# Moving the first loads of W_v to a second DMA queue, in a kernel for linear attention and a gated feed-forward layer

## The chip, the cores and the metric

The kernel runs on one core of a Trainium2 chip. A core has a matrix engine (TensorE, PE in the profile), a vector engine (VectorE, DVE), an engine for activation functions (ScalarE, ACT), a general one (GpSimd, POOL), and SyncE (SP), which here only issues DMA transfers. Each engine takes its instructions in order and they wait for each other through semaphores. SyncE and ScalarE each have a queue of DMA transfers; the transfers run on 16 DMA engines. The metric is the device time of one execution, in microseconds (us); smaller is better.

## The reference

One transformer layer on a sequence of 2048 rows of 640 numbers, in bf16: a layer norm, linear attention with 32 heads of 20 channels, a second layer norm and a gated feed-forward layer of width 1536.

```python
qkv = layernorm(x) @ wqkv                      # 640 x 1920, split into q, k, v
pq = einsum("bhsd,hdf->bhsf", q, w_phi)        # 20 x 20 for each head; the same for k
phi_q = concat(softmax(pq), softmax(-pq))      # 40 features for each head; the same for k
kv = einsum("bhsf,bhsd->bhfd", phi_k, v)
num = einsum("bhqf,bhfd->bhqd", phi_q, kv)
den = einsum("bhqf,bhf->bhq", phi_q, phi_k.sum over s) + 1e-6
h = x + (num / den) @ wo
out = h + (gelu(layernorm(h) @ w_gate) * (layernorm(h) @ w_up)) @ w_down
```

## The kernel before

The 2048 rows are 16 tiles of 128 rows; four tiles share one buffer `x_sb[b]`. A weight with 640 rows lies in SBUF as five chunks of 128 rows, so that W_v, the last third of `wqkv`, is `Wv[:, 0:5, :]`, each chunk 128 x 640 (160 KB, as is a tile of x).

The work comes in three stages: k and v of all tiles with the sums over the sequence (`kv_tile`), q and the attention's output, and the feed-forward layer. W_k and W_q are not used as they are: they are loaded transposed (`load_T`, `WkT`) and multiplied on TensorE with a block-diagonal matrix `BD` made from `w_phi` (`fold`), so that one product with the normalised x gives the features before the softmax. `BD` is made by one VectorE instruction (`bd`, L433) from `wphi` and a mask.

The order of the instructions on TensorE and SyncE is the order of the program text, and under a manual schedule around the whole kernel that of the other engines too. A DMA transfer signals one of eight semaphores, taken in turn by the order of the text; a transfer whose semaphore was used by an earlier one waits, on the issuing engine, until that one has landed.

The change is in the start. The first loads are at L189 to L198, then five transposing loads of W_k follow (L203). ScalarE issues one of them, `wphi`, and then loads its table of functions. TensorE meanwhile runs matmuls on constants (`warm`, L228). What follows is this:

- Tiles 0 and 1 are centred but not scaled (`xc`), transposed on TensorE (`tr_c`, into `LN1T`, copied by ScalarE at L165) and their scale, the reciprocal deviation, is applied later, when ScalarE moves v out of PSUM (`v_ev`, L316). The statistics of tile 0 are VectorE's (`ln_0`), those of tile 1 ScalarE's (`st_act`, L407 and L409).
- VectorE then takes the statistics of tile 2 (`ln_st(2)`), `BD`, the normalised tile 2 (`ln_ap(2)`, L156), the statistics of tile 3 with the copy of tile 2's transposes in between (`ln_st(3, between=...)`), and tile 3 after that.
- TensorE runs v of tiles 0 and 1 in parts (`v_part(t, chunks)`, L312, two matmuls of 320 columns for each chunk of W_v), with the transposes of tile 2 among them (`ln_tp(2, True)`, L164), then v of tile 2, the transposes of tile 3, and the five folds of W_k (L248), with v of tile 3 and parts of k in between.

The lines of the start that are concerned:

```python
439: st_act(1, 0)
440: xc = [ln_0(0)]
441: xc.append(xc_a(1))
442: tr_c(0)
443: tr_c(1)
444: ln_st(2, act=False, log=True)
445: bd(0, NC)
446: st_act(1, 1)
447: warm(*[P] * 4)
```

Of the kernel before, what the change touches and what calls it, by code (L numbers as in the profile page):

```python
# [17 lines left out]
def kernel(  # L18
# [12 lines left out]
    nc = tc.nc  # L31
    P = 128
    S = 2048
    D = 640
# [5 lines left out]
    NC = D // P  # L40
# [34 lines left out]
    w_v = A_wqkv.rearrange("(c p) n -> p c n", p=P)  # L75
    phi_v = A_w_phi.rearrange("h d f -> (h d) f")
# [9 lines left out]
    wphi = const.tile([P, NC, Dh], BF16, name="wphi")  # L86
# [24 lines left out]
    def gtile(name):  # L111
        return psG.tile([P, 2, 512], F32, name=name, tag="G")
# [63 lines left out]
    Wv = p1.tile([P, NC, D], BF16, name="Wv")  # L176
# [11 lines left out]
    nc.gpsimd.memset(eps, EPS)  # L188
    nc.sync.dma_start(x_sb[0][:, 0:1, :], x_v[:, 0:1, :])  # L189
    nc.sync.dma_start(x_sb[0][:, 1:2, :], x_v[:, 1:2, :])  # L190
    nc.scalar.dma_start(wphi, phi_v.rearrange("(c p) f -> p c f", p=P))
    nc.scalar.add_instruction(mybir.InstLoadActFuncSet(name=nc.get_next_instruction_name(), act_func_set_id=6))
    nc.sync.dma_start(x_sb[0][:, 2:3, :], x_v[:, 2:3, :])  # L193
    nc.sync.dma_start(Wv[:, 0:2, :], w_v[:, 0:2, 2 * D:3 * D])
    nc.sync.dma_start(Wv[:, 2:4, :], w_v[:, 2:4, 2 * D:3 * D])
    nc.sync.dma_start(x_sb[0][:, 3:4, :], x_v[:, 3:4, :])
    nc.sync.dma_start(Wv[:, 4:5, :], w_v[:, 4:5, 2 * D:3 * D])
    nc.sync.dma_start(x_sb[1][:, 0:2, :], x_v[:, 4:6, :])  # L198

    def load_T(WT, i, *ds):  # L200
# [25 lines left out]
    def warm(*cols):  # L226
        for n in cols:
            nc.tensor.matmul(wu[:, 0, 0:n], lhsT=ones[:, 0:P], rhs=ones[:, 0:n], start=True, stop=True)  # L228
# [46 lines left out]
    def ln_st(*tiles, act=True, between=None, log=False):  # L275
        for t, v in zip(tiles, ln_stats(p1, [x_sb[t // 4][:, t % 4, :] for t in tiles], "1", act, between, log)):
            lnp[t] = v

    def ln_ap(t, on_act=False, on_pe=False):
        ln = (ln_act if on_act else ln_dve)(p1, "1", *lnp[t])  # L280
        if on_pe:
            lnp[t] = ln
        else:
            transpose_to(LN1T[t // 4][:, :, t % 4 * P:(t % 4 + 1) * P], ln, False)

    def ln_tp(t, on_dve=False):
        transpose_to(LN1T[t // 4][:, :, t % 4 * P:(t % 4 + 1) * P], lnp[t], True, on_dve)

    def lnT(t, c):
        b, tl = divmod(t, 4)  # L290
        return LN1T[b][:, c, tl * P:(tl + 1) * P]
# [14 lines left out]
    def v_part(t, *cs):  # L306

        if 0 in cs:
            pv[t] = gtile("pv")
        for c in cs:  # L310
            for u in range(2):
                nc.tensor.matmul(pv[t][:, u, 0:HD], lhsT=lnT(t, c), rhs=Wv[:, c, u * HD:(u + 1) * HD],  # L312
                                 start=(c == 0), stop=(c == NC - 1))

    def v_ev(t):
        nc.scalar.activation(vS[t % NV][:, :, 1:VC].rearrange("p (u h) f -> p u h f", u=2),  # L316
                             pv[t][:, :, 0:HD].rearrange("p u (h f) -> p u h f", f=Dh), ACTF.Copy,
                             scale=lnp[t][2] if t in CT else 1.0)
# [126 lines left out]
    bd(0, NC)  # L445
    st_act(1, 1)
    warm(*[P] * 4)
    v_part(0, 0, 1)
    v_part(1, 0, 1)
    ln_ap(2, on_pe=True)  # L450
    v_part(0, 2, 3)
    root = []
    ln_st(3, act=False, between=lambda: ln_tp(2, True), log=root)
    v_part(0, 4)
    v_ev(0)
    v_part(1, 2, 3)
    root[0]()
    v_part(1, 4)
    v_ev(1)
    v_part(2, *range(NC))  # L460
    d = ident.rearrange("p (r j) -> p r j", r=4)
# [476 lines left out]
```

## Time and profile before

| | us |
|---|---|
| median of 3 runs | 272.64 |
| lowest and highest | 271.77, 272.8 |
| the profiled execution | 272.35 |
| its span, first to last instruction | 270.6 |
| TensorE busy in it | 266.1 |

The costliest group of matmuls is that of the feed-forward layer (L768, 600 matmuls). The start, with which this document deals, is the first 17 us of the span; the granted clock of TensorE is 1.00 of full speed in all the stretches shown. Times in the profile count from the start of the span. A line of the timeline has the start, the length, the engine, the line of the program, the operation, what it writes and reads, and in brackets the idle time of its engine before it with what ended it. "SPq" and "ACTq" are the issues of transfers by SyncE and ScalarE; PEld is the loading of weights into TensorE.

### The profile page before, as it was taken

To read this page: it belongs to the slowest core of one execution; us is meant where nothing else is said; L and a number is where in the kernel's file an instruction comes from. 1 tells how busy PE (TensorE), PEld (TensorE's weight loads), DVE (VectorE), ACT (ScalarE), POOL (GpSimd) and SP (SyncE) were. 2 spreads that over 40 slices of the span, in tenths; PEclk is the share of its full clock that TensorE was granted. 3 is DMA by queue.
4 is the path that set the end of the run, shared out by engine and by line. 5 is a ranking of instruction groups with operands and counts; after the bars stand their busy time and mean duration, and the time that the engine had idled before them with its cause. 6 is when DMAs were issued, how large, how long until landed. Compare 5 with 4: busy or idle time off the path is not lost.

```text
span 270.6 us, 7029 instructions
## 1 busy us (share of the span) xinstructions
PE 266.1 (98%) x2857; PEld 172.0 (64%) x2857; DVE 173.9 (64%) x347; ACT 138.6 (51%) x249; POOL 101.2 (37%) x238
## 2 busy tenths in 40 slices
PE   8999999999999999999999999999999999999995
PEld 6777777765455887788755455775555476444574
DVE  5789999996877767876566783568673332333322
ACT  5779997877789675245541356421544300322100
POOL 5448898887002335376211564014661100000000
DMA  6987489213864442432301222203222101000011
GB/s 187 206 199 169 81 210 96 46 37 85 326 201 112 157 101 55 68 78 50 51 27 51 48 50 48 50 3 75 76 46 51 24 24 51 24 0 0 4 48 48
DMA packets 45264, 22.10 MB, mean 82 GB/s; under 512 B 37808, under 2 KB 43184, under 8 KB 45232
## 3 DMA queue, kind: packets, MB, share of 16 engines
q1 hardware_dynamic: 44576, 21.64, 33.5%
q8 instruction: 22, 0.36, 0.6%
q10 hardware_dynamic: 656, 0.03, 0.2%
q14 instruction: 10, 0.08, 0.1%
HBM read 10.18 MB, written 2.62 MB: 47 GB/s over the span
## 4 chain that ended last, share of the span: by engine, by line
PE 96%; DMA 2%; SPq 0%; DVE 0%; issue 0%
PE gu L768 39%; PE pd L790 19%; PE pq L396 8%; PE pk L296 8%; PE po L708 8%; PE pv L296 7%; DMA Wv<-in_A_wqkv_dram 2%; PE kvp L374 2%; PE pv L312 2%; PE ab L619 1%; PE wa L248 1%; PE ab L586 1%; PE tp L164 0%; SPq L193 0%; SPq L190 0%; SPq L189 0%
## 5 line engine op out<-in xcount | busy, mean ns | idle before, releaser
L771 ACT ACTIVATE g<-gu 128x512 bf16<-128x512 f32 (+1 forms) x60 | 30.4, 510 | 74.0 <-PE gu L768 73.2
L774 DVE TENSOR_TENSOR GT<-gu,g 128x512 bf16<-128x512 f32 (+1 forms) x60 | 34.3, 579 | 46.8 <-PE gu L768 38.6
L768 PE MATMUL gu<-LN2T,Wg 128*128 128x512 bf16 (+1 forms) x300 | 61.8, 337 | 0.0
L768 PE MATMUL gu<-LN2T,Wu 128*128 128x512 bf16 (+1 forms) x300 | 61.8, 336 | 0.0
L790 PE MATMUL pd<-Wd,GT 128*128 128x320 bf16 (+4 forms) x396 | 53.9, 295 | 0.0
L790 PEld LDWEIGHTS <-GT 128*128 128x128 bf16 x396 | 37.6, 98 | 14.5 <-DVE GT L774 0.2
L768 PEld LDWEIGHTS <-Wu 128*128 128x128 bf16 x300 | 29.4, 98 | 22.6
L768 PEld LDWEIGHTS <-Wg 128*128 128x128 bf16 x300 | 29.1, 98 | 21.2
L296 PEld LDWEIGHTS <-LN1T 128*128 128x128 bf16 x290 | 28.0, 98 | 10.4
L355 POOL TENSOR_TENSOR E<-E,rs 128x640 bf16<-128x640 bf16 x25 | 31.7, 1295 | 4.4 <-DVE rs L351 2.8
L792 DVE TENSOR_TENSOR y<-pd,x_sb 128x320 bf16<-128x320 f32 (+4 forms) x33 | 15.8, 480 | 24.1 <-PE pd L790 24.1
L708 PE MATMUL po<-Wo,oT 128*128 128x320 bf16 x160 | 24.5, 299 | 0.0
L296 PE MATMUL pk<-Wk,LN1T 128*128 128x320 bf16 x160 | 24.4, 299 | 0.0
L396 PE MATMUL pq<-LN1T,Wq 128*128 128x512 bf16 x100 | 22.9, 379 | 0.0
L347 DVE TENSOR_REDUCE sk<-E 128x64 f32<-128x1280 bf16 x16 | 22.9, 1430 | 0.0
L401 ACT ACTIVATE Eq<-pq 128x1024 bf16<-128x1024 f32 (+1 forms) x26 | 19.9, 831 | 2.8 <-PE pq L396 2.7
L340 ACT ACTIVATE E<-pk 128x640 bf16<-128x640 f32 x28 | 19.1, 769 | 3.0 <-PE pk L296 3.0
L708 PEld LDWEIGHTS <-oT 128*128 128x128 bf16 x160 | 15.6, 98 | 7.3 <-ACT oT L165 0.2
L296 PE MATMUL pv<-Wv,LN1T 128*128 128x320 bf16 x130 | 19.8, 299 | 0.0
L151 ACT ACTIVATE ln<-x_sb,v,rstd 128x640 bf16<-128x640 bf16 x14 | 12.9, 920 | 13.0 <-POOL v L747 12.9
L396 PEld LDWEIGHTS <-Wq 128*128 128x128 bf16 x100 | 9.4, 98 | 10.3
L683 DVE TENSOR_TENSOR tt<-AB,w 128x1280 bf16<-128x1280 f32 x10 | 15.1, 1505 | 0.4 <-POOL w L676 0.3
(120 smaller groups left out, 291.4 us busy)
## 6 DMA issues: line engine op xcount, KB each, us to landing
out_dram<-y SPq DMA_DIRECT2D x15, 160.0 KB, 1.8
x_sb<-in_A_x_dram SPq DMA_DIRECT2D x6, 320.0 KB, 3.3
Wd<-in_B_w_down_dram SPq DMA_DIRECT2D x1, 1440.0 KB, 6.8
Wg<-in_B_w_gate_dram SPq DMA_DIRECT2D x1, 1152.0 KB, 7.3
Wu<-in_B_w_up_dram SPq DMA_DIRECT2D x1, 1152.0 KB, 5.6
Wo<-in_A_wo_dram SPq DMA_DIRECT2D x1, 800.0 KB, 5.0
Wg<-in_B_w_gate_dram SPq DMA_DIRECT2D x1, 768.0 KB
Wu<-in_B_w_up_dram SPq DMA_DIRECT2D x1, 768.0 KB, 9.1
```

Source lines behind the costliest of these rows:

```text
L296: nc.tensor.matmul(ps[:, u, 0:HD], lhsT=lnT(t, c), rhs=W[:, c, u * HD:(u + 1) * HD], start=(c == 0), stop=(c == NC - 1))
L340: nc.scalar.activation(Ek[t][:, s, :].rearrange("p (u f) -> p u f", u=2), pk[:, :, 0:HD], ACTF.Exp, scale=((lnp[t][2], nrstd[t]) if t in C ...
L347: nc.vector.reduce_sum(sk, Ek[t].rearrange("p s (h f) -> p (s h) f", f=Dh), axis=AX.X)
L355: eng.tensor_tensor(e, e, rs[:, s * H:(s + 1) * H, None].to_broadcast([P, H, Dh]), ALU.mult)
L396: nc.tensor.matmul(pqs[j][:, i, :], lhsT=Wq2[:, kc, c * P:(c + 1) * P], rhs=LN1T[b][:, kc, :], start=(kc == 0), stop=(kc == NC - 1))
L401: nc.scalar.activation(Eq[j][:, :, s, :], pqs[j][:, 0:len(QG[j])], ACTF.Exp, scale=(1.0, -1.0)[s])
L708: nc.tensor.matmul(pos[u], lhsT=st[t][:, c, :], rhs=Wo[:, c, u * HD:(u + 1) * HD], start=(c == 0), stop=(c == NC - 1))
L768: nc.tensor.matmul(gu[i][:, 0:n], lhsT=W[:, c, f * P:(f + 1) * P], rhs=LN2T[b][:, c, a0:a1], start=(c == 0), stop=(c == NC - 1))
L771: nc.scalar.activation(g[:, 0:n], gu[0][:, 0:n], ACTF.Gelu_apprx_tanh)
L774: nc.vector.tensor_tensor(st[b, "g", f][:, a0:a1], gu[1][:, 0:n], g[:, 0:n], ALU.mult)
L790: nc.tensor.matmul(pd[:, 0:f1 - f0], lhsT=st[b, "g", f][:, tl * P:(tl + 1) * P], rhs=Wd[:, f, f0:f1], start=(f == 0), stop=(f == NF - 1), ...
L792: nc.vector.tensor_tensor(y[:, f0:f1], pd[:, 0:f1 - f0], x_sb[b][:, tl, f0:f1], ALU.add)
```

## The change

Two things change. ScalarE issues the first four chunks of W_v, in two transfers, instead of `wphi`; SyncE issues x tiles 0, 1 and 2, the last chunk of W_v, `wphi`, tile 3 and the rows of tiles 4 and 5. And TensorE takes all five chunks of v of tile 0 ahead of v of tile 1, with tile 0's `v_ev` right after it. The number of instructions and of bytes is the same; SyncE issues one transfer fewer, ScalarE one more.

```diff
     nc.sync.dma_start(x_sb[0][:, 0:1, :], x_v[:, 0:1, :])
     nc.sync.dma_start(x_sb[0][:, 1:2, :], x_v[:, 1:2, :])
-    nc.scalar.dma_start(wphi, phi_v.rearrange("(c p) f -> p c f", p=P))
+    nc.scalar.dma_start(Wv[:, 0:2, :], w_v[:, 0:2, 2 * D:3 * D])
+    nc.scalar.dma_start(Wv[:, 2:4, :], w_v[:, 2:4, 2 * D:3 * D])
     nc.scalar.add_instruction(mybir.InstLoadActFuncSet(name=nc.get_next_instruction_name(), act_func_set_id=6))
     nc.sync.dma_start(x_sb[0][:, 2:3, :], x_v[:, 2:3, :])
-    nc.sync.dma_start(Wv[:, 0:2, :], w_v[:, 0:2, 2 * D:3 * D])
-    nc.sync.dma_start(Wv[:, 2:4, :], w_v[:, 2:4, 2 * D:3 * D])
+    nc.sync.dma_start(Wv[:, 4:5, :], w_v[:, 4:5, 2 * D:3 * D])
+    nc.sync.dma_start(wphi, phi_v.rearrange("(c p) f -> p c f", p=P))
     nc.sync.dma_start(x_sb[0][:, 3:4, :], x_v[:, 3:4, :])
-    nc.sync.dma_start(Wv[:, 4:5, :], w_v[:, 4:5, 2 * D:3 * D])
     nc.sync.dma_start(x_sb[1][:, 0:2, :], x_v[:, 4:6, :])
```

```diff
     warm(*[P] * 4)
-    v_part(0, 0, 1)
+    v_part(0, *range(NC))
+    v_ev(0)
     v_part(1, 0, 1)
     ln_ap(2, on_pe=True)
-    v_part(0, 2, 3)
     root = []
     ln_st(3, act=False, between=lambda: ln_tp(2, True), log=root)
-    v_part(0, 4)
-    v_ev(0)
-    v_part(1, 2, 3)
+    v_part(1, 2, 3, 4)
     root[0]()
-    v_part(1, 4)
     v_ev(1)
     v_part(2, *range(NC))
```

## The prediction

> **What bounds the kernel now.** I read the page first (busy time, chain that ended last), then TensorE's waits, the chain in order of time, and the timeline of the first 17 us.
>
> ```profile
> span 270.6 us, 7029 instructions
> PE 266.1 (98%) x2857; PEld 172.0 (64%) x2857; DVE 173.9 (64%) x347; ACT 138.6 (51%) x249; POOL 101.2 (37%) x238
> ```
>
> ```profile
> PE pv L312 <- DMA Wv<-in_A_wqkv_dram: 0.9, 1, 0.9
> PE wu L228 <- PEq L922: 0.8, 1, 0.8
> ```
>
> TensorE is busy for 98% of the span and waits twice: 0.8 us for the program to begin and 0.9 us for the first chunks of W_v. The second wait is all that an earlier W_v can remove. The chain in order of time (start, length, what) shows the place, and that TensorE sets the end from there on:
>
> ```profile
> 2.18 5.18 DMA Wv<-in_A_wqkv_dram
> 7.36 0.04 issue
> 7.41 1.79 PE pv L312 x12
> 9.20 0.28 PE tp L164 x5
> 9.47 2.44 PE pv L312 x18
> 11.92 0.28 PE tp L164 x5
> 12.20 0.98 PE wa L248 x18
> ```
>
> So the first chunks, issued fourth on SyncE at 2.18, landed at 7.36. From 7.41 every piece begins where the last ended; whatever is late to one of these pieces by less than TensorE moves up costs nothing, and what is later eats the gain.
>
> **What stands before the v matmuls.** The timeline (start, length, engine, line; in brackets the idle time before) of x tiles 0 and 1:
>
> ```profile
> 1.28 1.28 ACT L192 ACT_TABLE_LOAD   x1 [1.28 <-PEq L922]
> 3.27 0.89 DVE L121 BATCH_NORM_STATS2 statsc<-x_sb 128x6 f32<-128x320 bf16 x2 [0.64 <-DMA x_sb<-in_A_x_dram]
> 4.01 0.74 ACT L407 ACTIVATE sqa<-x_sb 128x640 bf16<-128x640 bf16 x1 [1.44 <-DMA x_sb<-in_A_x_dram]
> 4.87 0.39 DVE L424 TENSOR_SCALAR xc<-x_sb,va 128x640 bf16<-128x640 bf16 x1
> 5.63 1.29 ACT L165 COPY LN1T<-tp 128x640 bf16<-128x640 bf16 x2 [0.37 <-PE tp L164]
> 5.92 0.63 PE L228 MATMUL wu<-const-bfloat16-1.0 128*128 128x128 bf16 x4
> ```
>
> Tile 1 landed at 4.01. ScalarE's statistic of tile 1 stands in its queue ahead of tile 0's copy, and TensorE transposes both tiles and runs four warm-up matmuls, until 6.55 (5.92 + 0.63), before the first v matmul. So v starts no sooner than 2.54 us after tile 1 lands, and no sooner than W_v.
>
> **The change, part by part.**
>
> *ScalarE's queue.* One issue more there (some 0.48 us, as on SyncE) moves the table load from 1.28 to about 1.76, ending at 3.04; ScalarE's next work began at 4.01. Hidden; without that 0.97 us of cover it would cost its 0.48.
>
> *The start of v.* 320 KB of W_v now travel beside x tiles 0 and 1, and w_phi no longer does. The rates of the transfers (last two columns: busy DMA engines as a share, GB/s), and w_phi's queue in the first 4 us:
>
> ```profile
> 1.75:2.50 0.75, 0.75 (x10) 0.75 (x9) 0.45 (x6) 0.75 (x1) 0.61 (x5) 1.00 0.73 176
> 2.50:3.50 1.00, 1.00 (x12) 1.00 (x11) 0.32 (x2) 0.07 (x1) 0.80 (x6) 1.00 1.13 268
> 3.50:5.00 1.50, 1.45 (x15) 1.19 (x13) 1.38 (x5) 0.99 (x3) 0.63 (x13) 1.00 0.79 195
> 5.00:7.50 2.50, 1.65 (x15) 1.48 (x15) 2.15 (x6) 2.07 (x7) 0.52 (x2) 1.00 1.00 336
> ```
>
> ```profile
> q10 hardware_dynamic: 656, 0.03, 11.2%
> ```
>
> W_v's 327,680 bytes at 336 GB/s are 0.98 us; w_phi's 656 small packets are 11.2% of 4 us, 0.45 us. Tile 1 therefore lands between 0.45 earlier (W_v fills only gaps; the share of 0.73 to 0.79 shows that there are some) and 0.98 later (no gap is filled, no credit). I take 0.98 - 0.45 = 0.53 later, since both transfers have the same size and start together: 4.54, and v at 4.54 + 2.54 = 7.08, 0.33 us sooner than 7.41. The bounds are 6.1 (in truth 6.55, as tile 0 has its own chain) and 7.53. All the later W_v chunks are wanted 0.5 and 1.1 us after that, and stand ahead of w_phi, whose landing is treated next.
>
> The Trainium skill (DMA: Bandwidth & Descriptors, "Issuing engines are not separate DMA queues") speaks against the change: transfers from different engines run on the same 16 DMA engines and interleave, so that issuing from two saves only the issue time. Taken at its strictest it gives the upper bound for tile 1, v at 7.53, and nothing gained at this place. No row of before can show it, as only w_phi came from ScalarE.
>
> *w_phi.* BD needs it, and BD stands in VectorE's queue ahead of the normalised tile 2, the statistics of tile 3 and all that follows:
>
> ```profile
> 6.62 0.94 DVE L433 TENSOR_TENSOR BD<-wphi,hmask 128x800 bf16<-128x800 bf16 x1
> 7.48 0.44 DVE L156 TENSOR_SCALAR ln<-x_sb,mv,rstd 128x640 bf16<-128x640 bf16 x1
> 8.61 0.49 DVE L121 BATCH_NORM_STATS2 stats<-x_sb 128x6 f32<-128x320 bf16 x1 [0.68 <-DMA x_sb<-in_A_x_dram]
> 9.51 0.49 DVE L165 COPY LN1T<-tp 128x640 bf16<-128x640 bf16 x1 [0.41 <-PE tp L164]
> 9.92 0.48 DVE L121 BATCH_NORM_STATS2 stats<-x_sb 128x6 f32<-128x320 bf16 x1
> 10.44 0.21 DVE L125 BATCH_NORM_AGGREGATE mv<-stats 128x2 f32<-128x12 f32 x1
> 11.25 0.45 DVE L156 TENSOR_SCALAR ln<-x_sb,mv,rstd 128x640 bf16<-128x640 bf16 x1 [0.24 <-ACT rstd L132]
> 11.76 0.45 PE L164 MATMUL tp<-ident,ln 128*128 128x128 bf16 x5
> 12.26 0.48 DVE L165 COPY LN1T<-tp 128x640 bf16<-128x640 bf16 x1
> ```
>
> ```profile
> wphi<-in_A_w_phi_dram ACTq DMA_DIRECT2D x1, 25.0 KB, 2.8
> ```
>
> Before, w_phi landed 2.8 after its issue at 0.79, by 3.6, three microseconds early. Now it is fifth on SyncE, behind x tiles 0 to 2 and the last chunk, while ScalarE's queue carries four more: 1280 KB are ahead of it or beside it, exactly what stood up to x tile 3 before (three tiles, four chunks, a tile), which landed at 8.61. With the same use of the DMA engines w_phi lands at 8.61: the upper bound. For the lower bound I stream from 2.5 at 336 GB/s, after 132 KB (0.75 us at 176): 1.34 MB are through at 6.1, and with the 0.8 that tile 1 needed (its and tile 0's 328 KB were through by about 3.2 at the rates above, against 4.01) 6.9. I take the middle, 7.75.
>
> From w_phi's landing W to tile 3's transposes, by differences of starts above: BD 0.86, tile 2's ln 0.44 and 0.05 to its transposes, 0.50 to its copy (11.76 to 12.26), 0.41 to the second statistic, 0.52 to the aggregate, 0.81 to tile 3's ln, 0.51 to its transposes: W + 4.10. For 7.75 that is 11.85. TensorE would be there at 7.08 + (11.76 - 7.41) = 11.43. So it waits 0.42, and the 0.33 won is more than returned: it stands 0.09 later than before. W = 7.66 is break-even.
>
> *SyncE's queue.* In the built program the DMAs share eight semaphores in turn, so the ninth transfer, x rows 4 and 5 (L198 in both), waits until the first on its semaphore has landed. Before, that was w_phi (3.6, and SyncE came to it at 4.15: no stall). Now it is W_v's first pair, and the five W_k transposes stand behind it:
>
> ```profile
> 4.15 0.43 SPq L198 DMA_DIRECT2D x_sb<-in_A_x_dram  x1
> 4.63 7.69 SPq L203 DMA_TRANSPOSE WkT<-in_A_wqkv_dram  x5
> 15.65 0.43 PEld L248 LDWEIGHTS <-WkT 128*128 128x128 bf16 x6
> ```
>
> ```profile
> 11.04 1.28 SPq L203 DMA_TRANSPOSE WkT<-in_A_wqkv_dram  x1
> ```
>
> ```profile
> WkT<-in_A_wqkv_dram SPq DMA_TRANSPOSE x1, 4.5
> ```
>
> ```profile
> L203 SPq DMA_TRANSPOSE WkT<-in_A_wqkv_dram x5: 1266/1276/1891, 4.6 to 11.0; - x5
> ```
>
> The last transpose, issued at 11.04, lands 4.5 later at 15.54, and its weights are loaded at 15.65: 0.11 us of slack. One issue fewer would bring SyncE to L198 at 3.67. If W_v's pair lands at 4.99 (4.01 + 0.98, the bytes of both tiles and of the pair; bounds: 4.01, as fast as two tiles alone, and 0.79 + 5.18 = 5.97, its present time from issue), L198 is 0.84 later than at 4.15. Of the 7.69 us for five transposes, 5 x 1.28 + 4 x 0.05 = 6.6 are needed; 1.1 are in longer issues, which I read as full rings that a later start relieves. So the last transpose shifts by -0.26 to +0.84; I take the middle, +0.3: 15.84, and 0.19 us of TensorE's time.
>
> *Sum.* The stalls follow each other on one engine, so the last one decides: of -0.33 at the start of v, +0.09 at tile 3 and +0.19 at the last fold, +0.19 is left. The profiled execution took 272.35 (1.75 outside the span): 272.54. It lies 0.29 below the median of 272.64; I say 272.6.
>
> The order of v itself (tile 0 whole, then tile 1) costs nothing: the same 20 matmuls, and 14 rather than 12 of them ahead of tile 2's transposes, which favours a late tile 2 by 0.27 us (2 x 0.136, from 18 in 2.44); this is in the W chain.
>
> **Rivals.**
> 1. *The gain is kept.* x and W_v fill each other's gaps, w_phi lands by 7.0, the last transpose lands 0.26 sooner or more: v at 7.0 to 6.55, and 0.37 (0.11 of slack and 0.26) to 0.86 off: 271.5 to 272.0, say 271.75. For it: shares of 0.73 and 0.79 while nothing else held the engines. Against it: the skill's rule, and that three gates must open together. Chance 0.2.
> 2. *w_phi is late* (other side): at 8.61 tile 3's transposes come at 12.71, 0.95 late: 273.3. It decides from 7.66 on. Against it: two queues may use the engines better. Chance 0.2.
> 3. *SyncE stalls behind W_v's pair* (other side): at 5.97 and no relief, the transposes shift by 1.82, the last fold waits 1.71: 274.05. It decides from 4.26 on without relief, 5.4 with it. Against it: the pair is alone in its queue. Chance 0.2.
>
> **How the numbers follow.** The forecast has 0.4, and a range of its own of 272.2 to 273.0 (the ends of the shift at the last fold). The range of 271.6 to 274.1 takes in most of rival 1, rival 2, and half of rival 3. Half a per cent, about what a measurement of this kernel can tell from no change, is 1.36 us. Faster by that (under 271.28) is out of reach of 0.86 us off 272.35 but for scatter: 0.04. Slower by it (over 274.0) needs rival 3 at its upper end, or rivals 2 and 3 together: 0.18. The rest, 0.78, is within.
>
> **What would show it.** TensorE's wait for W_v of 0.9 gone or under 0.3; L407's wait for x longer than 1.44 and its start near 4.5; BD starting at 7.75 with a wait for w_phi; TensorE waiting some 0.4 us at tile 2's or 3's transposes; SyncE idle ahead of L198 till about 5; the last fold late. If BD starts by 7.0 and the fold's weights are there, I am wrong towards rival 1; if tile 1 lands past 5, the start of v itself is a loss.

## The result, and the profile after

The changed kernel is slower. Over all runs of this measurement, 6 of each:

| | before | changed |
|---|---|---|
| median, us | 271.84 | 274.05 |
| lowest and highest | 271.57, 272.8 | 273.62, 275.62 |
| span of the profiled execution | 270.6 | 273.9 |

The ratio is 1.0095, with a 95% interval of 1.0072 to 1.0118: 2.2 us by the medians. The six runs fall into two groups: four of 273.6 to 274.1 and two of 275.5 and 275.6. The profiled one is of the second group (275.62), so it shows one thing that most runs do not have.

TensorE's waits in the profile of the changed kernel (who waited for whom, us in total, times, longest):

```profile
PE pd L787 <- DVE GT L771: 1.3, 1, 1.3
PE wu L228 <- PEq L919: 0.8, 1, 0.8
PE tp L164 <- DVE xc L272: 0.7, 1, 0.7
PE tp L164 <- DVE xc L424: 0.2, 1, 0.2
```

The wait for W_v is gone. Two small waits ahead of the transposes of tiles 0 and 1 have come, and a wait of 1.3 us at a place that no line of the diff touches: the first matmul of the down projection (`pd`), some 100 us later. It waits for `GT`, which VectorE makes from the gate and up products `gu`. The same place in the kernel before, then in the changed kernel:

```profile
103.69 2.62 PE L790 MATMUL pd<-Wd,GT 128*128 128x326 bf16 x18
```

```profile
106.92 2.62 PE L787 MATMUL pd<-Wd,GT 128*128 128x326 bf16 x18 [1.33 <-DVE GT L771]
```

Here is TensorE's timeline of the start:

```profile
5.49 0.72 PE L164 MATMUL tp<-ident,xc 128*128 128x128 bf16 x5 [0.67 <-DVE xc L272]
6.41 0.71 PE L164 MATMUL tp<-ident,xc 128*128 128x128 bf16 x5 [0.20 <-DVE xc L424]
6.92 0.63 PE L228 MATMUL wu<-const-bfloat16-1.0 128*128 128x128 bf16 x4
7.34 3.46 PE L312 MATMUL pv<-Wv,LN1T 128*128 128x320 bf16 x14
10.64 0.44 PE L164 MATMUL tp<-ident,ln 128*128 128x128 bf16 x5
10.92 2.34 PE L312 MATMUL pv<-Wv,LN1T 128*128 128x320 bf16 x16
13.36 0.45 PE L164 MATMUL tp<-ident,ln 128*128 128x128 bf16 x5
```

v starts at 7.34, where it started before (7.41). But its first 14 matmuls take 3.46 us, against 2.34 for the 16 that follow, and tile 3's transposes come at 13.36, not 11.76: 1.60 late. The durations of one v matmul, as least, median and most ns, say why (the kernel before first):

```profile
L312 PE MATMUL pv<-Wv,LN1T x30: 296/299/299, 7.4 to 11.6; 128*128 128x320 bf16 x30
```

```profile
L312 PE MATMUL pv<-Wv,LN1T x30: 299/299/474, 7.3 to 13.0; 128*128 128x320 bf16 x30
```

474 ns where the others take 299: in this run TensorE was still at its slow rate, as in the warm-up (matmuls of 128 columns take 311 ns there, and also in the transposes and the four warm-up matmuls right ahead of v; at the full rate they take about 220). The granted clock in the profile stands at 1.00 all the same.

What is behind the waits for xc is the loads. The timeline of the changed kernel (SPq and ACTq are issues):

```profile
0.79 0.46 ACTq L191 DMA_DIRECT2D Wv<-in_A_wqkv_dram  x1
1.28 0.49 ACTq L192 DMA_DIRECT2D Wv<-in_A_wqkv_dram  x1
3.88 0.89 DVE L121 BATCH_NORM_STATS2 statsc<-x_sb 128x6 f32<-128x320 bf16 x2 [1.25 <-DMA x_sb<-in_A_x_dram]
4.69 0.33 SPq L198 DMA_DIRECT2D x_sb<-in_A_x_dram  x1
5.10 0.74 ACT L407 ACTIVATE sqa<-x_sb 128x640 bf16<-128x640 bf16 x1 [2.02 <-DMA x_sb<-in_A_x_dram]
7.45 0.94 DVE L433 TENSOR_TENSOR BD<-wphi,hmask 128x800 bf16<-128x800 bf16 x1
```

Tile 0 lands 0.6 later than before (3.88 against 3.27) and tile 1 1.1 later (5.10 against 4.01). SyncE is held at L198 until W_v's first pair has landed, at 4.69. BD runs at 7.45 without a wait for w_phi.

### The profile page after: what moved, and what is told of

Read it like the earlier page. It is cut to its first block, busy times and chain, and to the rows that moved or that the text cites. A ratio compares the mean times of both kernels' runs of the same rounds, so it can differ in the third digit from the quotient of the medians.

```text
span 273.9 us, 7029 instructions
## 1 busy us (share of the span) xinstructions
PE 267.9 (98%) x2857; PEld 172.5 (63%) x2857; DVE 174.1 (64%) x347; ACT 138.8 (51%) x249; POOL 101.4 (37%) x238
## 4 chain that ended last, share of the span: by engine, by line
PE 95%; DVE 2%; DMA 1%; issue 1%; ACT 0%; SPq 0%
PE gu L765 37%; PE pd L787 19%; PE pq L396 8%; PE pk L296 8%; PE po L705 8%; PE pv L296 6%; PE kvp L374 2%; DMA x_sb<-in_A_x_dram 1%; PE ab L616 1%; PE pv L312 1%; PE wa L248 1%; PE ab L583 1%; PE tp L164 1%; DVE tt L680 1%; DVE GT L771 0%
## 5 line engine op out<-in xcount | busy, mean ns | idle before, releaser
L296 PEld LDWEIGHTS <-LN1T 128*128 128x128 bf16 x290 | 28.0, 98 | 10.4
L340 ACT ACTIVATE E<-pk 128x640 bf16<-128x640 f32 x28 | 18.5, 729 | 3.2 <-PE pk L296 3.2
```

Source lines behind the costliest of these rows:

```text
L296: nc.tensor.matmul(ps[:, u, 0:HD], lhsT=lnT(t, c), rhs=W[:, c, u * HD:(u + 1) * HD], start=(c == 0), stop=(c == NC - 1))
L340: nc.scalar.activation(Ek[t][:, s, :].rearrange("p (u f) -> p u f", u=2), pk[:, :, 0:HD], ACTF.Exp, scale=((lnp[t][2], nrstd[t]) if t in C ...
```

## The experiments

Each ran beside the kernel before on the same chip. "High" counts the runs more than 1.2 us above the lowest run of the same kernel; the kernel before has 7 such runs of 89 itself. The ratio is not that of the two medians, so the two can differ by some 0.1 to 0.2%.

| run | median, us | before beside it | ratio, 95% interval | high |
|---|---|---|---|---|
| changed kernel | 274.05 | 271.84 | 1.0095 (1.0072 to 1.0118) | 2 of 6 |
| e1, last chunk after tile 2 | 272.22 | 271.66 | 1.0038 (1.0022 to 1.0054) | 4 of 12 |
| e2, loads only | 272.17 | 271.66 | 1.0019 (1.0007 to 1.0032) | 1 of 11 |
| e3, order only | 274.19 | 271.66 | 1.0092 (1.0079 to 1.0105) | 0 of 4 |
| e4, longer warm-up | 273.75 | 271.66 | 1.0076 (1.0063 to 1.0089) | 0 of 5 |
| g1, changed, other PSUM tile | 272.33 | 271.54 | 1.0024 (0.9998 to 1.005) | 2 of 11 |
| g2, before, other PSUM tile | 273.1 | 271.54 | 1.0049 (1.0031 to 1.0068) | 0 of 11 |
| g3, x split over queues | 271.83 | 271.54 | 1.0007 (0.9988 to 1.0026) | 0 of 11 |
| g4, changed, both mended | 272.32 | 271.54 | 1.0023 (1.0004 to 1.0041) | 0 of 11 |
| h1, table before W_v | 272.85 | 271.94 | 1.0035 (1.0014 to 1.0057) | 6 of 12 |
| h2, W_v after the table | 272.58 | 271.88 | 1.0029 (1.0016 to 1.0042) | 0 of 6 |

**Where the wait at pd comes from.** The built programs of before and after differ there in one number, the count of VectorE's semaphore that the first pd matmul waits for. Each line names the PSUM bank that it writes and the count; "later" are the counts at which the last two `GT` are done, for which before only later matmuls wait:

```
before  pd  bank 0  waits DVE >= 158      later: GT waits DVE >= 162, 163
after   pd  bank 0  waits DVE >= 163
```

163 is the last GT, 158 one that is done long before. The reason is which PSUM buffer each tile is dealt. Until `split()`, a call in the program text shortly ahead of that place, four buffers of two banks rotate, and a tile takes the one that is given back first; after it there are eight buffers of one bank. When v of tile 0 is taken whole, its buffer is given back before that of tile 2's transposes, not after; from there on two buffers have changed places. So, some 100 us later, the last gate/up tile `gu` stands in banks 0 and 1 in the changed kernel, and in banks 2 and 3 before; and the first pd tile takes bank 0, which is not free until VectorE has read `gu` to make the last GT. The first two experiments part the loads from the order.

`e1_last_chunk_after_tile2`, the changed kernel with two matmuls moved:

```diff
-    v_part(0, *range(NC))
-    v_ev(0)
+    v_part(0, 0, 1, 2, 3)
     v_part(1, 0, 1)
     ...
     ln_st(3, act=False, between=lambda: ln_tp(2, True), log=root)
+    v_part(0, 4)
+    v_ev(0)
     v_part(1, 2, 3, 4)
```

> The changed kernel, except that chunk 4 of v of tile 0 (two matmuls) and its eviction come after the transposes of tile 2. In the built program this puts the PSUM buffers back as they were before: the first down-projection matmul (pd) waits for an earlier GT instead of the last one. Theory A (part of the loss is a wait of the first pd matmul for the last GT, made by a swap of two PSUM buffers at the start): the wait of 1.33 us of pd for GT is gone, and the time falls by about 1.3 us from 274.05, to 272.5 to 273.0. Rival B (all of the loss is at the start: late x, half clock): the wait does not matter or comes back elsewhere, and the time stays at 273.7 to 274.3.

272.22, and in its profile the wait of pd is gone:

```profile
PE wu L228 <- PEq L920: 0.8, 1, 0.8
PE tp L164 <- DVE xc L424: 0.4, 1, 0.4
PE tp L164 <- DVE xc L272: 0.3, 1, 0.3
```

1.8 us less than the changed kernel (1.65 if each is measured from the kernel before beside it), by a place for two matmuls: theory A, and somewhat more than it expected. Four of its twelve runs are 1.4 to 1.8 us higher.

`e2_loads_only` and `e3_order_only` take the two hunks of the diff apart: the new L189 to L198 with the old order of v, and the old loads with the new order.

> The new order of the loads with the old order of v. Theory A: no wait of pd for GT, x tile 1 lands near 5.1 as in the changed kernel, so that only the start is lost: 272.3 to 273.0, with single runs up to 274 where TensorE stays at half rate in the v matmuls (474 ns instead of 299). Rival B: the loads are the whole loss, 274.0 like the changed kernel.

> The old order of the loads with the new order of v (tile 0 whole first). Theory A: the wait of 1.3 us of pd for GT is there although no load was moved; v of tile 0 may also wait some tenths for the last chunk of W_v, which landed at 9.0 and is wanted at 8.5: 273.2 to 273.7, v matmuls at 299 ns. Rival B: as before, 271.8 to 272.3.

The loads alone cost 0.5 us (272.17, 0.1 below what was expected), and the order alone, with no load moved, costs as much as the whole change (274.19, a ratio of 1.0092 against 1.0095). e3's waits show where:

```profile
PE pd L787 <- DVE GT L771: 1.3, 1, 1.3
PE wu L228 <- PEq L919: 0.8, 1, 0.8
PE pv L312 <- ACT LN1T L165: 0.7, 1, 0.7
PE tp L164 <- DVE xc L272: 0.4, 1, 0.4
PE pv L312 <- DMA Wv<-in_A_wqkv_dram: 0.2, 1, 0.2
```

The same wait at pd, and one for the last chunk of W_v, which with the old loads lands too late for a tile 0 that is taken whole. e3 came out above what was expected, by some 0.5. Its chain in order of time, from tile 2's transposes, has a further part of that (pieces of issue of 0.02 to 0.04 us are left out):

```profile
9.34 0.29 PE tp L164 x5
9.66 0.49 DVE LN1T L165
10.15 0.41 DVE stats L121
10.58 0.22 DVE mv L125
10.83 0.30 ACT ve L131
11.16 0.21 ACT rstd L132
11.39 0.46 DVE ln L156
11.90 0.45 PE tp L164 x5
```

From tile 2's transposes to tile 3's the end is set here by VectorE's and ScalarE's chain, not by TensorE. The stretch takes 2.7 us in every profile (9.03 to 11.76 before, 10.64 to 13.36 after). The old order has 18 v matmuls in that stretch, 2.44 us by its chain, and the 0.28 of the transposes: exactly as long. The new order has put two of them ahead, so that TensorE is idle for about their 0.27. From v's first matmul to tile 3's transposes it is 4.35 us before and in g2 (both below), with the old order, and 4.63 in e4, g1 and g4, with the new one; e1, e2 and h1, with the old order and late x, lie between (4.53 to 4.56).

**The same edit, on both kernels.** If only the dealing of buffers counts, an edit that moves no work should be able to mend the changed kernel and to break the old one. In both, the four warm-up matmuls ahead of v got a PSUM tile of their own:

```diff
-    warm(*[P] * 4)
+    warm(*[P] * 4, w=gtile("wu"))
```

In the built programs the first pd matmul now waits for count 158 in the changed kernel and for 163 in the kernel before.

> The changed kernel; the four warm-up matmuls ahead of v write a PSUM tile of their own instead of the shared one. No load and no step of v is moved; in the built program the PSUM buffers of all later tiles are dealt out otherwise, and the first down-projection matmul waits for an earlier GT (not the last). Theory A (the order of v cost 1.5 us only through the dealing of PSUM buffers): no wait of pd for GT, about 1.5 us less than the changed kernel: median 272.3 to 272.8, single runs 1.5 above that where the v matmuls are at half rate. Rival B (taking tile 0 whole costs by itself): 273.5 to 274.2.

> The kernel before with the same edit and nothing else. Here the built program's first down-projection matmul now waits for the last GT. Theory A: the wait of 1.3 us of pd for GT appears, and the kernel is 1.5 us slower than before although the change of this case is not in it: 273.0 to 273.4. Rival B: 271.5 to 271.9.

272.33 and 273.1: the edit takes 1.7 us off the changed kernel (1.4 if each is measured from the kernel before beside it) and puts 1.56 on the kernel before. g2 has the wait at pd that the kernel before lacks:

```profile
PE pd L790 <- DVE GT L774: 1.3, 1, 1.3
PE wu L228 <- PEq L922: 0.8, 1, 0.8
PE pv L312 <- ACT LN1T L165: 0.6, 1, 0.6
```

Rival B falls on both sides. g2's profile tells something about the kernel before as well: with before's loads and order v here waits 0.6 for its transposed x and not for W_v. So does e3, with the same loads: its first v matmul, at 6.68, waits 0.7 for x. The wait of 0.9 for the first chunks of W_v, on which the prediction was built, is thus in one of the three profiles with the old loads, that of an execution of 272.35, where most runs of the kernel lie near 271.6. No second execution of the kernel before itself was profiled.

**The slow rate.** e4 is the changed kernel with TensorE kept busy in its two waits ahead of the transposes:

```diff
-    warm(*[512] * 2, *[P] * 28)
+    warm(*[512] * 2, *[P] * 34)
...
     tr_c(0)
+    warm(*[P] * 4)
     tr_c(1)
```

> The changed kernel with 10 more warm-up matmuls: 6 at the end of the first series and 4 between the transposes of tile 0 and of tile 1, which fill TensorE's waits of 0.7 and 0.2 us. Theory C (in some runs TensorE's rate stays at half until about 10.5 us because of these idle times): all v matmuls at 299 ns, no run above 274.3, the wait of pd for GT still there, median 273.5 to 274.0. Rival D (the rate rises at a moment that has nothing to do with these gaps): single runs still near 275.5 and v matmuls at 474 ns in some profiles, median 274.0 or more.

273.75, with all five runs within 0.2 us; its v matmuls:

```profile
L312 PE MATMUL pv<-Wv,LN1T x30: 299/299/310, 6.8 to 11.0; 128*128 128x320 bf16 x30
```

g4 adds g1's edit to it.

> The changed kernel with the longer warm-up (10 more matmuls) and the four matmuls ahead of v in a PSUM tile of their own. Theory A and C together: no wait of pd for GT, v at 299 ns in all runs, x tile 1 still late: 272.2 to 272.5, with no run above 272.8; what is left against before (0.5 to 0.8 us) is the start. Rival: a further loss shows, over 273.

272.32 and no high run in eleven. With the new loads on both queues and no filled gaps, 15 of 52 runs were high (changed kernel, e1, e2, g1, h1); with filled gaps none of 16 (and none of 6 in h2, below, where W_v comes later). That bears out theory C, but does not close it: the five runs of e4 alone would not tell, the kernel before has some high runs too, and only one profile has matmuls at 474 ns; no second high run was profiled. Nor do the gaps alone make a run slow: e2 and g1 wait as long ahead of the transposes (0.8 and 0.5 us, 1.0 and 0.5), and their profiles have the transposes at 221 ns and v at 299. The Trainium skill (TensorE: Matmul & The Clock Gate, "The HAM clock gate") says that TensorE runs at half rate until it has been busy through one window of about 3.4 us, and that the windows run free, so that it depends on the run in which of them a gap falls. This agrees with two groups of runs. The size of the loss is the profile's: 14 matmuls in 3.46 us, where e4, g1 and g4 take 2.08, are 1.4 us, and the groups are 1.4 to 1.8 us apart.

**What the loads cost.** g3 keeps the old order of v and puts x on both queues.

```diff
     nc.sync.dma_start(x_sb[0][:, 0:1, :], x_v[:, 0:1, :])
-    nc.sync.dma_start(x_sb[0][:, 1:2, :], x_v[:, 1:2, :])
-    nc.scalar.dma_start(wphi, ...)
+    nc.scalar.dma_start(x_sb[0][:, 1:2, :], x_v[:, 1:2, :])
+    nc.scalar.dma_start(x_sb[0][:, 2:3, :], x_v[:, 2:3, :])
     nc.scalar.add_instruction(mybir.InstLoadActFuncSet(...))
-    nc.sync.dma_start(x_sb[0][:, 2:3, :], x_v[:, 2:3, :])
     nc.sync.dma_start(Wv[:, 0:2, :], ...)
+    nc.sync.dma_start(wphi, ...)
     nc.sync.dma_start(Wv[:, 2:4, :], ...)
     nc.sync.dma_start(x_sb[0][:, 3:4, :], ...)
```

> The order of v of before; loads: SyncE x tile 0, W_v 0:2, w_phi, W_v 2:4, x tile 3, W_v 4:5; ScalarE x tiles 1 and 2, then its table. If the two queues take turns by whole transfers (x tile 1 landed 0.8 to 1.1 later behind W_v in the runs with W_v on ScalarE), tile 1 lands at about 3.5 instead of 4.0 and W_v 0:2 by 5: v starts at 6.1 to 6.4 (6.7 in a run of before's loads without a late W_v), 0.3 to 0.6 us faster than before: 271.1 to 271.4. If the queues share evenly or tile 0 is what counts, no gain: 271.5 to 271.9.

271.83, no gain: tile 1 was there at 3.86 (4.01 before), but tile 0, which now shared the DMA engines with it, only at 3.68 (3.27 before), and TensorE waited 0.5 us for it.

In h1 ScalarE's table load stands ahead of its two W_v issues in the text.

> The new loads with the old order of v, and ScalarE's table load (1.28 us) ahead of its two W_v issues, so that W_v is issued at about 2.1 to 2.6 instead of 0.79. If the loss of the loads (0.5 us) is that the x tiles stand behind whole W_v transfers of the other queue, x tiles 0 and 1 land as in the kernel before (by 3.3 and 4.0 to 4.2), and the time is that of before or a little under, 271.3 to 271.8, with no v matmul at half rate. If the loss lies elsewhere (SyncE's wait at L198, w_phi behind W_v), it stays at 272.0 to 272.3, or grows, as SyncE waits longer for W_v.

The edit did not do what it was made for. The timeline has the issues at the old times, while the table is being loaded:

```profile
0.79 1.28 ACT L191 ACT_TABLE_LOAD   x1 [0.79 <-PEq L922]
0.82 0.45 ACTq L192 DMA_DIRECT2D Wv<-in_A_wqkv_dram  x1
```

So it says nothing on the question; it is nearly e2 again, with six high runs of twelve (one of eleven in e2), which is why its median stands 0.9 above the kernel before. One more thing differs: the eight semaphores follow the order of the built program, which changed, so that SyncE now waits for x tiles 0 and 1 (L198 until 3.88) and not for W_v. h2 delays the issues by a real dependence: a small ScalarE instruction writes into `Wv`, and the transfers wait for it. Its edit against h1:

```diff
     nc.scalar.add_instruction(mybir.InstLoadActFuncSet(...))
+    nc.scalar.activation(Wv[:, 0:4, 0:1], nc.const_aps.tensor(1.0, [P, 4], BF16)[:, :, None], ACTF.Identity)
     nc.scalar.dma_start(Wv[:, 0:2, :], ...)
```

> The new loads with the old order of v; ScalarE writes one element of each of the first four W_v chunks once its table is loaded, and its W_v transfers wait for that, so that they are issued at about 2.4 and 2.9 instead of 0.8 and 1.3. If W_v's whole transfers ahead of x are the loss of the loads, x tile 0 lands by 3.3 and tile 1 by 4.0 to 4.2, TensorE has no wait at tile 0's transposes above 0.3, v starts at 6.5 to 7.0 and the time is that of before within 0.3 us, no run at half rate in v but for the odd one that before has too. If not, the time stays 0.5 above before.

```profile
2.33 0.43 ACTq L193 DMA_DIRECT2D Wv<-in_A_wqkv_dram  x1
3.12 0.89 DVE L121 BATCH_NORM_STATS2 statsc<-x_sb 128x6 f32<-128x320 bf16 x2 [0.49 <-DMA x_sb<-in_A_x_dram]
3.58 0.74 ACT L408 ACTIVATE sqa<-x_sb 128x640 bf16<-128x640 bf16 x1 [1.28 <-DMA x_sb<-in_A_x_dram]
6.70 1.82 PE L313 MATMUL pv<-Wv,LN1T 128*128 128x320 bf16 x12 [1.00 <-DMA Wv<-in_A_wqkv_dram]
7.88 0.99 DVE L434 TENSOR_TENSOR BD<-wphi,hmask 128x800 bf16<-128x800 bf16 x1 [1.42 <-DMA wphi<-in_A_w_phi_dram]
9.28 0.45 PE L164 MATMUL tp<-ident,ln 128*128 128x128 bf16 x5 [0.76 <-DVE ln L156]
12.02 0.44 PE L164 MATMUL tp<-ident,ln 128*128 128x128 bf16 x5
```

The half about x is right: issued 1.5 later, W_v lets tile 0 land by 3.12 and tile 1 by 3.58, both sooner than in the kernel before, so that it was the early W_v that kept them. The half about the time is wrong: 272.58, not better. w_phi, issued by SyncE at 2.65 as in the changed kernel, is now there only at 7.88, BD waits 1.42 for it, and TensorE waits 0.76 for tile 2. No order of these loads that was tried beat the old one, and no version beat the kernel before.

## Why the prediction was wrong

*The step that failed* is the one it spent least on: "The order of v itself (tile 0 whole, then tile 1) costs nothing". It cost the larger part. Of the 2.2 us between the medians, 1.4 (changed kernel against g1) to 1.56 (g2 against before) are the wait at pd, 1.33 in the profiles, and about 0.3 the missing cover between tile 2 and tile 3, where the prediction had put down a help of 0.27. The rest is the 0.5 of the loads (e2); these shares come from separate runs and add up to 2.2 to 2.4. The prediction looked for what the order does at its place. What it changes of the dealing of PSUM buffers stood in the built program as another wait count, and was not looked at.

*The start of v.* Here 0.33 sooner was forecast, by tile 1 landing at 4.54. It landed at 5.10, beyond the upper bound of 4.99; in the six other profiles with the same early W_v it is 4.79 to 5.43, against 3.97 to 4.03 in the three with the old loads. The transfers had been taken as sharing evenly. Two stretches of half a microsecond in the changed kernel show that they do not (packets, MB, and share of the 16 engines; q10 is ScalarE's queue, q1 SyncE's), the first from 3.25 us:

```profile
q10 hardware_dynamic: 145, 0.18, 98.5%
q1 hardware_dynamic: 15, 0.02, 8.6%
```

and the second from 3.75:

```profile
q1 hardware_dynamic: 91, 0.11, 60.8%
q10 hardware_dynamic: 78, 0.08, 46.1%
```

In the first, ScalarE's queue has nearly everything, in the second about half. Tile 1 came 0.41 to 0.45 us after W_v's first pair in all six profiles in which SyncE's wait shows when that landed (5.10 after 4.69 in the changed kernel): it stood behind the whole pair. The strictest reading of the Trainium skill's rule, which the prediction gave as the bound, was nearer than the value that it took. The other term was too long: v began 2.24 us after tile 1 in the changed kernel and 1.88 to 1.89 after it in the six other profiles, not 2.54: in the profile of before the ten transposes and the four warm-up matmuls, which that term takes in, ran at the slow rate (308 and 311 ns, against 221 and 220 in e2). So 7.34, close to the forecast of 7.08, comes of two errors in opposite directions. Nor is it a gain: before's 7.41 was the late W_v of one execution, and v starts at 6.58 and 6.68 in the two other profiles with the old loads (g2, e3).

*w_phi* was the opposite case. Forecast for 7.75, with 6.9 as the least, it landed 4.5 us after its issue at 2.65, at about 7.15:

```profile
wphi<-in_A_w_phi_dram SPq DMA_DIRECT2D x1, 25.0 KB, 4.5
```

BD, at 7.45, did not wait for it. The middle was too late because the transfers used the DMA engines better between 3.50 and 5.00 (394 GB/s, against 195 before), though not from the start (61 against 176 from 1.75 to 2.50). Rival 2 did not happen in the changed kernel; it did in h2, where W = 7.88 gave tile 3's transposes at 12.02, against W + 4.10 = 11.98 by the prediction's sum.

*SyncE's wait* at L198 came as described, until 4.69 (forecast 4.99), and cost nothing, though it was the term that decided the forecast, with 0.19 us. The five transposes of W_k behind it took 6.57 us (5.07 to 11.64) and not 7.69, so that the last one was issued at 10.4, sooner than before (11.04), and no fold waited. The relief that the prediction allowed for thus came in full; that full rings were its reason is shown by no run. Rival 3 named the right wait and the wrong price: that its 274.05 is also the measured median, and that the range's end of 274.1 takes the median in, is luck.

*The half rate* was in no step. The prediction let TensorE's work ahead of v slide by half a microsecond and did not ask what an idle TensorE does to the rate of what follows. The slow rate costs about 1.4 us in some runs; that it comes of these waits is likely by the spread of the runs, not proved.

## What to carry to other kernels

An edit of the order near the start of a program can change the dealing of rotating buffers for the rest of it; compare the wait counts of the two built programs all the way down, not only the order of the instructions, and look where one pool of buffers hands its banks to another. Before the gain of a wait is counted, see in a second execution whether the wait is there at all: this one was missing in both other profiles with the same loads. And a large load that a second queue issues at once can come ahead of the second load of the first queue, here by its whole length; issuing it 1.5 us later (h2) let x through sooner, but then a load behind it was late. Putting what is wanted first into both queues (g3) brought nothing here.

## What was not expected of the hardware

Two queues that are both full are not mixed evenly at every moment: 145 of 160 packets were ScalarE's in one stretch of half a microsecond, and 78 of 169 in the next. The Trainium skill (DMA: Bandwidth & Descriptors, "Queues, rings and completion order") has the engines change between queues after a whole packet of several descriptors. Uneven stretches fit that; the turns of a single engine are not in the profile.

ScalarE issues DMA transfers while its table is being loaded (0.82 in h1, with a load from 0.79 for 1.28 us); their place behind it in the text did not hold them back.
